# A delta-rule attention, a gated mixer and a channel mixer in one kernel: u blocks of w_in rounded in the second period, w_out and w_k later, mixing with delayed low parts

## Chip, cores, metric

The kernel runs on one core of one Trainium2 chip. The metric is the device time of one execution in microseconds (us). TensorE is called PE, VectorE DVE, ScalarE ACT, GpSimd POOL; SP only issues transfers here.

## What is computed

Three layers follow one another, for 4 sequences of 768 tokens and 384 channels (8 heads of 48). Cut to what matters:

```python
# 1: delta rule, token by token, per sequence and head
k_n = k / (np.linalg.norm(k, axis=-1, keepdims=True) + 1e-06)
for t in range(S):
    y[:, :, t] = einsum('bhd,bhde->bhe', q[:, :, t], state)
    v_old = einsum('bhde,bhd->bhe', state, k_n[:, :, t])
    state += beta[:, :, t] * einsum('bhd,bhe->bhde', k_n[:, :, t], v[:, :, t] - v_old)
# 2: x is y as (4, 768, 384); u, v halves of 512
u, v = split(gelu(x @ w_in))
v_s = einsum('ts,bsd->btd', w_sg, layernorm(v) * g_ln) + b_sg[None, :, None]
x = x + (u * v_s) @ w_out
# 3: x_prev is x one token earlier
k = relu((mu_k * x + (1 - mu_k) * x_prev) @ w_k)
r = sigmoid((mu_r * x + (1 - mu_r) * x_prev) @ w_r)
out = r * ((k * k) @ w_v)
```

## The kernel before, in words

**Products in two parts.** From the second layer on, each matrix is split into a high part (rounded to the type that PE multiplies) and a low part (the remainder), and a product is three matmuls: high by high, high by low, low by high (`mm3`, line 151). The weights arrive as pairs of 32-bit words. `narrow` (from line 154) makes a block of them into numbers: a load into one of three `raw` buffers (SP, line 160), a conversion on ACT (line 164), four bit operations on DVE into one of two `na` buffers (lines 169, 171, 173, 175, here called the rounding), an addition on POOL (177); `split` then copies the high part on ACT (120) and subtracts on POOL (123). The two `na` buffers come free when the subtraction is done. Six blocks of 128x256 belong to the v half of w_in and six to the u half; they stay on the chip. The blocks of w_out (eight, 192 wide) and w_k (twelve, 256 wide), later of w_r and w_v, are put back to memory in rounded form and read again in the third layer or the mixing.

**First layer.** Twelve steps `s` of 64 tokens are done in six groups, the periods; two steps each, and each step in two halves `o` of the channels. A period needs a triangular solve, `solver(g)` (lines 358 to 440), nearly all on DVE; it ends with a transpose into `DT` (line 440) and runs one period ahead of its use. `couple` (line 456) is PE's first product with `DT`; behind it come `st_d` (line 521, which also needs DVE's `residual`, line 475), ACT's copy `u` (526), `st_n` (534), and `st_rq`, `st_s`, `st_y` (498, 549, 563). ACT copies between them (540, 555), and 513 with a selection on POOL (514); `st_y` ends in ACT's copy `yst` (568) and six stores into `xT` (583, 588). The second layer's x @ w_in runs between the steps as `fill` (635 for v, 687 for u); where there is none, `keep_warm` issues matmuls without use (726).

**Who orders the work.** PE, ACT, DVE and POOL run in the order in which the program is written out until the third layer begins; SP's order is set by a scheduler up to the mixing. In the first layer a planner writes the order: a period has 24 ticks (`point[0]` counts them, from 0 after the first solve). `tick` starts jobs (a job is the rounding of one block): a `while` as long as more than `n_rest` jobs, that is blocks of w_in, remain and fewer than RUN[0] run, and an `if` for one job every EVERY ticks with at most RUN[1] running. `background` deals out the DVE time of a tick (BUDGET) among layer norm, solver and jobs in the ratio SHARE[point[1]]; each stream pays its time divided by its share.

**Mixing.** For four sequences and two halves `t` of the tokens, a slice `d` (of four) is 18 matmuls (line 960) into one PSUM bank, two operations on DVE (1056, 1058) and a split into `gh`, `gl`; `project` (1064) multiplies with w_out. `side(n)` works off up to n steps of the remaining rounding jobs; up to three run, a new one from the turns in `starts` on (a turn is a slice). Between the slices `load_v` splits the next sequence's v into the ring that PE reads.

Of the kernel before, what the change touches and what calls it, by code (L numbers as in the profile page):

```python
# [7 lines left out]
F32 = mybir.dt.float32  # L8
# [3 lines left out]
AF = mybir.ActivationFunctionType  # L12
ALU = mybir.AluOpType
# [23 lines left out]
PRE = 0.8  # L37
GRAM0 = 7
SOLVE0 = 1
RUN = (3, 2, 3)  # L40
SUMS = (0,)
EVERY = 6
LATE = 100
PUT = 2
JLAG = 2
# [9 lines left out]
LASTP = 134  # L55
# [2 lines left out]
COST = dict(rq=1.05, d=0.8, n=0.8, s=0.85, y=1.1)  # L58
INST = dict(rq=128, d=128, n=64, s=64, y=64)
PACE = 0.0157  # L60
SHARE = ((1, 12, 1), (1, 4, 1), (2, 8, 2))
NRAW = 3
NNA = 2
PD = 2
SD = 1
CS = (5, 4)
VF = (0, 3)
VD = 1
# [18 lines left out]
def fused_kernel(  # L87
# [18 lines left out]
    V, A, G, T = nc.vector, nc.scalar, nc.gpsimd, nc.tensor  # L106
# [10 lines left out]
    def split(eng_hi, eng_lo, src, hi, lo):  # L117

        if eng_hi is A:
            A.activation(hi, src, AF.Copy)  # L120
        else:
            eng_hi.tensor_scalar(hi, src, 1.0, None, op0=ALU.mult)
        eng_lo.tensor_tensor(lo, src, hi.bitcast(F32), op=ALU.subtract)  # L123
# [69 lines left out]
    def scratch(dram, name, nblk, n, cw=CW, pool=stg):  # L193

        d = dp.tile([nblk, P, 2, n], F32, name=name + "_d")

        def job(i, j):
            parts = []
            yield from narrow(dram, i, j, None, None, cw, pool, parts=parts)

            def put():
                nc.sync.dma_start(out=d[i, :, :, j:j + cw], in_=parts[0])

            yield PUT, put

        return d[:, :, 0], d[:, :, 1], [lambda i=i, j=j: job(i, j) for i in range(nblk) for j in range(0, n, cw)]
# [12 lines left out]
    wo_dh, wo_dl, jobs = scratch(w_out, "wo", 4, DM, DM // 2)  # L219
    wk_dh, wk_dl, j1 = scratch(w_k, "wk", 3, FF)  # L220
    jobs += j1
    n_rest = len(jobs)
# [26 lines left out]
    with ExitStack() as at:  # L249
# [70 lines left out]
        def gram(g, parts=((0, 64),)):  # L320

            GL = GLs[g] = GLb[g % 3]

            def half(i, c0, c1, j):
                t = kT[2 * g + i // 2]
                if j == 0:
                    GDs["ps"] = bank()
                gps = GDs["ps"]
                for p in range(4 * j, 4 * j + 4):
                    u = (i % 2) * 8 + p  # L330
                    for h in range(2):
                        r = 64 * (1 - h)
                        T.matmul(gps[r:r + 32, p, c0:c1], lhsT=t[r:r + 64, u, 0:32],  # L333
                                 rhs=t[r:r + 64, u, c0:c1], start=True, stop=True)
                        T.matmul(gps[r + 32:r + 64, p, c0:c1], lhsT=t[r:r + 64, u, 32:64],  # L335
                                 rhs=vw2(t, r, 64, u * C + 32 - c0, [(-32, (c1 - c0) // 32), (1, 32)]),
                                 start=True, stop=True)
                if j:
                    for x, c in ((GD[:, :, 8 * i:8 * i + 8].rearrange("p j u -> p u j"), 0),
                                 (GL[:, 8 * i:8 * i + 8, :], 32)):  # L340
                        if c0 <= c < c1:
                            A.activation(x, gps[:, :, c:c + 32], AF.Copy, scale=-1.0)

            GDs[g] = GD
            return [[(0, lambda i=i, j=j, c=c: half(i, *c, j)) for j in range(2)]
                    for c in parts for i in range(4)]
# [248 lines left out]
        later, vstat, streams, point = [], {}, [], [0, 0]  # L595
# [132 lines left out]
        def background(t):  # L728

            for e in [e for e in later if e[0] <= point[0]]:  # L730
                later.remove(e)
                e[1]()
            while splits and x_split(*splits[0]):
                splits.pop(0)
            t += debt[0]
            debt[0] = 0
            while t > 0:
                ready = [e for e in streams if e[0] <= point[0]]
                if not ready:
                    return  # L740
                kinds = [[e for e in ready if e[2] == k] for k in ("ln", "solve")]
                kinds.append([e for e in ready if any(e[1] is j for _, j in running[:2])])
                if not any(kinds):
                    return
                k = min((k for k in range(3) if kinds[k]), key=lambda k: spent[k])
                for j in range(3):
                    if not kinds[j]:
                        spent[j] = max(spent[j], spent[k])
                e = kinds[k][0]
                try:  # L750
                    c = next(e[1])
                    if isinstance(c, tuple):
                        e[0] = point[0] + c[0]
                        if c[0] == 0:
                            c[1]()
                        elif c[1] is not None:
                            after(c[0], c[1])
                    else:
                        t -= c
                        spent[k] += c / SHARE[point[1]][k]  # L760
                    streams.remove(e)
                    streams.append(e)
                except StopIteration:
                    streams.remove(e)
                    running[:] = [r for r in running if r[1] is not e[1]]
            debt[0] = min(t, 0) * (point[1] > 0)

        running, debt = [], [0]
        jobs = in_jobs + jobs
        n_jobs = len(jobs)  # L770

        def start_job(lead=LJ):
            j = jobs.pop(0)()
            running.append((n_jobs - len(jobs) - 1, j))
            next(j)
            streams.append([point[0] + lead, j, "job"])
# [58 lines left out]
        def tick():  # L835
            g, n = divmod(point[0], 24)
            point[1] = min(g, 1) + 1
            gg, nn = divmod(point[0] - GRAM0, 24)
            if nn == 0 and 0 <= gg and gg + 2 < NG:
                grams.extend(gram(gg + 2))  # L840
            if n == 0 and g + 1 < NG:
                streams.append([point[0] + SOLVE0, solver(g + 1), "solve"])
            late = point[0] >= LATE
            if point[0] < LASTP and jobs and len(running) < RUN[1 + late] and n % (2 if late else EVERY) == 0:
                start_job(LJ5 if late else LJ)
            background(BUDGET * (B0 if g == 0 else 1))
            while len(jobs) > n_rest and len(running) < RUN[0]:
                start_job()
            if grams and (point[0] - GRAM0) % GSTEP == 0:
                for _, f in grams.pop(0):  # L850
                    f()
                used[0] += 1.1
                dense[0] += 1
            point[0] += 1
# [152 lines left out]
    wr_dh, wr_dl, j2 = scratch(w_r, "wr", 3, DM, DM, st)  # L1007
    wv_dh, wv_dl, j3 = scratch(w_v, "wv", 8, DM, DM, st)
    jobs += j2 + j3
    live, turns, starts = [], [0], [1 + 2 * i for i in range(NRAW)]  # L1010

    def side(n):

        while n > 0:
            while jobs and any(x <= turns[0] for x in starts):
                starts.remove(next(x for x in starts if x <= turns[0]))
                j = jobs.pop(0)()
                next(j)
                live.append([turns[0] + 2, j, None])
            e = next((e for e in live if e[0] <= turns[0]), None)  # L1020
            if e is None:
                return
            if e[2]:
                e[2]()
            e[2] = None
            c = next(e[1], None)
            if c is None:
                live.remove(e)
                starts.append(turns[0] + 1)
            elif isinstance(c, tuple) and c[0]:  # L1030
                e[0], e[2] = turns[0] + 1, c[1]
            elif isinstance(c, tuple):
                c[1]()
            else:
                n -= 1

    halves = [(b, t) for b in range(B) for t in range(2)]
    us, gs = {}, {}
# [7 lines left out]
    def mix(b, t, d):  # L1046
        sl = slice(t * DM, t * DM + DM)
        pt, c0 = begun.pop(d, (None, 0))
        if pt is None:
            pt = ps.tile([P, HF], F32, name="ms")  # L1050
        for c in range(c0, 6):
            mix_mm(pt, b, t, d, c)
        if d == 0:
            gs[b, t] = [mp.tile([P, 4, DM], F32R, name=x) for x in ("gh", "gl")]
        w = vr.tile([P, DM], F32, name="w", bufs=2)
        V.scalar_tensor_tensor(w, pt[:, :DM], g_sb[:, d:d + 1], b_sb[:, sl],
                               op0=ALU.mult, op1=ALU.add)
        V.tensor_tensor(w, w, us[b, t][:, d], op=ALU.mult)  # L1058
        side(1)
        split(A, V, w, gs[b, t][0][:, d], gs[b, t][1][:, d])  # L1060
        side(SD)
        turns[0] += 1

# [173 lines left out]
```

## Time and profile before

| | us |
|---|---|
| median of 3 runs | 755.34 |
| lowest and highest run | 751.11, 757.25 |
| the profiled execution | 752.32 |
| its span in the profile | 750.3 |
| PE busy in the span | 690.7 (92%) |
| DVE, ACT, POOL busy | 510.8, 368.8, 202.4 |

All rows are from one profiled execution; their times count from the span's start. The execution's own time is 2 us above the span and 3.0 below the median. PE stood for 750.3 - 690.7 = 60 us of the span.

### The profile page before, as it was taken

The numbers are of one execution on the slowest core, as the hardware profiler recorded it, in microseconds if no ns is written. First come the engines' busy times: TensorE is split into PE (matmuls) and PEld (weight loads), VectorE is DVE, ScalarE is ACT, GpSimd is POOL, SyncE is SP. The second block draws the span as 40 slices with busy tenths as digits, with TensorE's granted clock in tenths as the row PEclk, the third lists the DMA queues.
The fourth block names the chain that finished last, engine by engine and source line by source line (L and its number), as shares of the span: only waits on it lengthen the run. The fifth ranks groups of instructions, "written<-read, shape, count | busy, mean of one in ns | idle before, by whom it ended". The sixth has DMA issues, their size and how long they took to land.

```text
span 750.3 us, 24940 instructions
## 1 busy us (share of the span) xinstructions
PE 690.7 (92%) x10832; PEld 640.4 (85%) x10832; DVE 510.8 (68%) x1070; ACT 368.8 (49%) x752; POOL 202.4 (27%) x253
## 2 busy tenths in 40 slices
PE   2568789999898999899989999999999999999998
PEld 2536568878776887779989999999999999999997
DVE  6989999878988795632494949489556564563341
ACT  2226656777666666874232313148445454452240
POOL 3033534454445355453133414420000000000000
PEclk9988989999999999999999999999999999999999
DMA  8503542674555565758755454195000000000000
GB/s 249 118 30 84 140 112 81 178 207 139 147 179 152 162 179 169 223 148 240 240 175 190 127 168 148 66 278 141 33 11 21 32 12 22 22 11 31 12 22 32
DMA packets 81549, 88.75 MB, mean 118 GB/s; under 512 B 24704, under 2 KB 64320, under 8 KB 81440
## 3 DMA queue, kind: packets, MB, share of 16 engines
q1 hardware_dynamic: 76384, 77.72, 35.1%
q0 software_dynamic: 5056, 9.44, 4.6%
q8 instruction: 85, 1.39, 0.8%
q14 instruction: 24, 0.20, 0.1%
HBM read 56.60 MB, written 25.82 MB: 110 GB/s over the span
## 4 chain that ended last, share of the span: by engine, by line
PE 73%; DVE 16%; DMA 4%; issue 3%; POOL 1%; SPq 1%; ACT 1%; POOLq 0%; DVEq 0%; ACTq 0%
PE ms L151 38%; PE ms L960 11%; PE ms L687 6%; PE ms L635 5%; DVE sg L355 4%; DVE sg L393 2%; PE ms L563 2%; PE rk L521 2%; PE sps L549 2%; PE ms L456 2%; PE rk L534 1%; PE rk L498 1%; PE ms L333 1%; PE ms L726 1%; DVE Yt L393 1%
## 5 line engine op out<-in xcount | busy, mean ns | idle before, releaser
L177 POOL TENSOR_TENSOR na<-na,raw 128x256 int32<-128x256 int32 (+2 forms) x43 | 36.4, 846 | 121.6 <-DVE na L175 53.5
L151 PE MATMUL ms<-wvh,sl 128*128 128x384 f32 x192 | 64.6, 336 | 0.0
L151 PE MATMUL ms<-wvl,sh 128*128 128x384 f32 x192 | 64.5, 336 | 0.0
L151 PE MATMUL ms<-wvh,sh 128*128 128x384 f32 x192 | 64.5, 336 | 0.0
L151 PE MATMUL ms<-xm_hi,sw0h 128*128 128x384 f32 x192 | 64.2, 335 | 0.0
L151 PE MATMUL ms<-xm_hi,sw0l 128*128 128x384 f32 x192 | 64.2, 334 | 0.0
L151 PE MATMUL ms<-xm_lo,sw0h 128*128 128x384 f32 x192 | 64.2, 334 | 0.0
L120 ACT ACTIVATE gh<-w 128x384 fp32r<-128x384 f32 x32 | 16.8, 525 | 94.9 <-DVE w L1058 94.9
L123 DVE TENSOR_TENSOR sl<-sg,sh 128x384 fp32r<-128x384 f32 x64 | 35.7, 558 | 30.2 <-ACT sh L120 30.2
L960 PE MATMUL ms<-sw0h,g 128*128 128x384 f32 x192 | 50.6, 336 | 3.0 <-ACT g L120 2.1
L120 ACT ACTIVATE sh<-sg 128x384 fp32r<-128x384 f32 x64 | 33.5, 524 | 35.9 <-DVE sg L1157 35.9
L960 PE MATMUL ms<-ws1h,g 128*128 128x384 f32 x192 | 49.9, 334 | 0.0
L355 DVE TENSOR_TENSOR sg<-sg,Yt 128x512 f32<-128x512 f32 (+10 forms) x78 | 46.7, 599 | 1.8
L1173 DVE TENSOR_TENSOR sg<-sg,ms 128x384 f32<-128x384 f32 x24 | 13.3, 554 | 45.3 <-PE ms L151 45.3
L1157 DVE TENSOR_TENSOR sg<-sg 128x384 f32<-128x384 f32 x64 | 35.5, 554 | 10.9 <-ACT sg L1156 10.9
L1156 ACT ACTIVATE sg<-ms 128x384 f32<-128x384 f32 x64 | 30.8, 481 | 23.7 <-PE ms L151 22.9
L514 POOL TENSOR_SCALAR_AFFINE_SELECT SQ<-SQ 64x512 f32<-64x512 f32 x36 | 27.5, 763 | 52.9 <-ACT SQ L513 51.7
L335 PE MATMUL ms<-kT 64*32 64x64 f32 (+1 forms) x640 | 23.3, 235 | 17.9 <-issue 17.9
L687 PE MATMUL ms<-xl,wiu_hi 128*128 128x256 f32 x144 | 39.7, 297 | 0.0
L687 PE MATMUL ms<-xh,wiu_lo 128*128 128x256 f32 x144 | 38.6, 291 | 0.9 <-issue 0.9
L333 PEld LDWEIGHTS ms<-kT 64*32 64x32 f32 x640 | 20.0, 131 | 22.2 <-issue 14.5
L120 ACT ACTIVATE xm_hi<-sg 128x384 fp32r<-128x384 f32 x48 | 23.3, 516 | 31.4 <-PE ms L151 30.5
(246 smaller groups left out, 2237.8 us busy)
## 6 DMA issues: line engine op xcount, KB each, us to landing
u_d<-ug SPq DMA_DIRECT2D x24, 256.0 KB, 3.8
u<-u_d SPq DMA_DIRECT2D x16, 384.0 KB, 4.6
vn_d<-v SPq DMA_DIRECT2D x22, 256.0 KB, 2.8
vk<-in_vk_dram SPq DMA_DIRECT2D x24, 192.0 KB, 4.0
vk<-in_vk_dram SPq DMA_DIRECT2D x12, 384.0 KB, 4.8
out_dram<-sg SPq DMA_DIRECT2D x24, 192.0 KB, 1.9
kT<-in_kt_d_dram SPq DMA_DIRECT2D x8, 512.0 KB, 5.8
SQ<-in_q_d_dram SPq DMA_DIRECT2D x36, 96.0 KB, 4.1
```

The costliest lines, as they stand in the source:

```text
L120: A.activation(hi, src, AF.Copy)
L123: eng_lo.tensor_tensor(lo, src, hi.bitcast(F32), op=ALU.subtract)
L151: T.matmul(pt, lhsT=a, rhs=b, start=(i == 0), stop=(i == n - 1))
L177: G.tensor_tensor(a.bitcast(I32), a.bitcast(I32), w_lo.bitcast(I32), op=ALU.add)
L333: T.matmul(gps[r:r + 32, p, c0:c1], lhsT=t[r:r + 64, u, 0:32], rhs=t[r:r + 64, u, c0:c1], start=True, stop=True)
L355: V.tensor_tensor(tv, vw(a_t, a_off, a_dims), vw(b_t, b_off, b_dims), op=ALU.mult)
L514: G.affine_select(out=pt, in_=pt, pattern=[[0, 8], [1, C]], compare_op=ALU.is_gt, fill=0.0, base=0, channel_multiplier=-1)
L635: T.matmul(vstat[g, b], lhsT=a[:, c], rhs=w[:, c], start=first, stop=last)
L687: T.matmul(vstat["u"][:, 2 * P * d:2 * P * d + 2 * P], lhsT=w[:, c, ds_], rhs=a[:, c].rearrange("p b t -> p (b t)"), start=first, stop=last)
L960: T.matmul(pt[:, :DM], lhsT=v[:, ds_], rhs=w, start=(c == 0 and i == 0), stop=(c == 5 and i == 2))
L1156: A.activation(r, pt[:, :DM], AF.Relu)
L1157: V.tensor_tensor(r, r, r, op=ALU.mult)
```

## The change

The u blocks of w_in are held back until tick 16 (the `while` keeps six jobs more until then); blocks of w_out and w_k start in the third period at the earliest, one every five ticks, with up to three jobs running. In the first period the solver's share rises from 4 to 8. In the mixing the high part is copied by ACT at once, the low part of a slice is subtracted one slice later (at once at the last slice of a sequence's second half), no rounding stands inside a slice any more, two steps of it stand behind each, and its first jobs start at turns 3, 4 and 6.

```diff
--- before.py
+++ after.py
@@ -37,9 +37,9 @@
 PRE = 0.8
 GRAM0 = 7
 SOLVE0 = 1
-RUN = (3, 2, 3)
+RUN = (3, 3, 3)
 SUMS = (0,)
-EVERY = 6
+EVERY = 5
 LATE = 100
 PUT = 2
 JLAG = 2
@@ -58,11 +58,11 @@
 COST = dict(rq=1.05, d=0.8, n=0.8, s=0.85, y=1.1)
 INST = dict(rq=128, d=128, n=64, s=64, y=64)
 PACE = 0.0157
-SHARE = ((1, 12, 1), (1, 4, 1), (2, 8, 2))
+SHARE = ((1, 12, 1), (1, 8, 1), (2, 8, 2))
 NRAW = 3
 NNA = 2
 PD = 2
-SD = 1
+SD = 2
 CS = (5, 4)
 VF = (0, 3)
 VD = 1
@@ -841,10 +841,10 @@
             if n == 0 and g + 1 < NG:
                 streams.append([point[0] + SOLVE0, solver(g + 1), "solve"])
             late = point[0] >= LATE
-            if point[0] < LASTP and jobs and len(running) < RUN[1 + late] and n % (2 if late else EVERY) == 0:
+            if g > 1 and point[0] < LASTP and jobs and len(running) < RUN[1 + late] and n % (2 if late else EVERY) == 0:
                 start_job(LJ5 if late else LJ)
             background(BUDGET * (B0 if g == 0 else 1))
-            while len(jobs) > n_rest and len(running) < RUN[0]:
+            while len(jobs) > n_rest + (0 if point[0] > 15 else 6) and len(running) < RUN[0]:
                 start_job()
             if grams and (point[0] - GRAM0) % GSTEP == 0:
                 for _, f in grams.pop(0):
@@ -1007,7 +1007,7 @@
     wr_dh, wr_dl, j2 = scratch(w_r, "wr", 3, DM, DM, st)
     wv_dh, wv_dl, j3 = scratch(w_v, "wv", 8, DM, DM, st)
     jobs += j2 + j3
-    live, turns, starts = [], [0], [1 + 2 * i for i in range(NRAW)]
+    live, turns, starts, owing = [], [0], [3, 4, 6], []
 
     def side(n):
 
@@ -1026,7 +1026,7 @@
             c = next(e[1], None)
             if c is None:
                 live.remove(e)
-                starts.append(turns[0] + 1)
+                starts.append(turns[0])
             elif isinstance(c, tuple) and c[0]:
                 e[0], e[2] = turns[0] + 1, c[1]
             elif isinstance(c, tuple):
@@ -1056,8 +1056,14 @@
         V.scalar_tensor_tensor(w, pt[:, :DM], g_sb[:, d:d + 1], b_sb[:, sl],
                                op0=ALU.mult, op1=ALU.add)
         V.tensor_tensor(w, w, us[b, t][:, d], op=ALU.mult)
-        side(1)
-        split(A, V, w, gs[b, t][0][:, d], gs[b, t][1][:, d])
+        A.activation(gs[b, t][0][:, d], w, AF.Copy)
+        if owing:
+            owing.pop()()
+        owing.append(lambda h=gs[b, t][0][:, d], l=gs[b, t][1][:, d]: V.tensor_tensor(
+            l, w, h.bitcast(F32), op=ALU.subtract))
+        if t == 1 and d == 3:
+            side(1)
+            owing.pop()()
         side(SD)
         turns[0] += 1
 
```

DVE, the end of solver 1: line 440 gives `couple` its operand, line 475 is the residual for `st_d` of step 2, line 360 begins solver 2; 169 to 175 on `na` are rounding. Before:

```order
L393 TENSOR_REDUCE sg_110<-sg_111 128x4x16
L173 TENSOR_SCALAR na<-na 128x256
L440 STREAM_TRANSPOSE DT<-sg_110 128x32x32
L169 TENSOR_SCALAR na<-raw 128x256
L175 SCALAR_TENSOR_TENSOR na<-raw,na 128x256
L475 TENSOR_TENSOR r_1642<-vk,rk 128x384
L171 TENSOR_SCALAR na<-na 128x256
L173 TENSOR_SCALAR na<-na 128x256
L175 SCALAR_TENSOR_TENSOR na<-raw,na 128x256
L360 STREAM_TRANSPOSE sg_108<-sg_109 128x1024
L364 TENSOR_SCALAR ss<-sg_108 128x32
```

Now, from line 440 to the same residual:

```order
L440 STREAM_TRANSPOSE DT<-sg_110 128x32x32
L171 TENSOR_SCALAR na<-na 128x256 x2
L173 TENSOR_SCALAR na<-na 128x256 x2
L175 SCALAR_TENSOR_TENSOR na<-raw,na 128x256 x2
L169 TENSOR_SCALAR na<-raw 128x256
L171 TENSOR_SCALAR na<-na 128x256
L173 TENSOR_SCALAR na<-na 128x256
L175 SCALAR_TENSOR_TENSOR na<-raw,na 128x256
L169 TENSOR_SCALAR na<-raw 128x256 x2
L171 TENSOR_SCALAR na<-na 128x256 x2
L173 TENSOR_SCALAR na<-na 128x256 x2
L475 TENSOR_TENSOR r_1634<-vk,rk 128x384
```

Two rounding instructions stood between lines 440 and 475; now there are 16. In the whole of solver 1 ahead of line 440 there were 21, and 4 are left. Behind the residual follow two 175, then 169, 171 and 173 of the last u block, and line 360.

SP, the same place: loads `raw` are weight blocks, the four kinds of `xT<-yst` are stores of `st_y` of step 1. Before, and then now:

```order
L160 DMA raw<-in_w_in_dram 128x512
L160 DMA raw<-in_w_out_dram 128x384
L279 DMA SQ_123<-in_q_d_dram 48x8x64
L279 DMA SQ_124<-in_q_d_dram 48x8x64
L583 DMA xT<-yst 48x6x128 x2
L588 DMA xT<-yst 32x2x128
L588 DMA xT<-yst 16x2x128 x2
L588 DMA xT<-yst 32x2x128
L160 DMA raw<-in_w_out_dram 128x384 x2
```

```order
L267 DMA kT_96<-in_kt_d_dram 128x1024
L279 DMA SQ_123<-in_q_d_dram 48x8x64
L279 DMA SQ_124<-in_q_d_dram 48x8x64
L583 DMA xT<-yst 48x6x128 x2
L588 DMA xT<-yst 32x2x128
L588 DMA xT<-yst 16x2x128 x2
L588 DMA xT<-yst 32x2x128
L160 DMA raw<-in_w_in_dram 128x512 x3
L160 DMA raw<-in_w_out_dram 128x384 x2
```

The loads of the last three u blocks have moved behind the stores.

DVE in the mixing of the first sequence, second half, from its second slice's 1056 to the first addition of `project`; `gl` is the low part, `g<-stw` a ring piece. Before, and then now:

```order
L1056 SCALAR_TENSOR_TENSOR w<-ms,g_sb,b_sb 128x384
L1058 TENSOR_TENSOR w<-w,u 128x384
L169 TENSOR_SCALAR na<-raw 128x384
L123 TENSOR_TENSOR gl<-w,gh 128x384
L171 TENSOR_SCALAR na<-na 128x384
L123 TENSOR_TENSOR g_7054<-stw,g_7054 128x512
L1056 SCALAR_TENSOR_TENSOR w<-ms,g_sb,b_sb 128x384
L1058 TENSOR_TENSOR w<-w,u 128x384
L173 TENSOR_SCALAR na<-na 128x384
L123 TENSOR_TENSOR gl<-w,gh 128x384
L175 SCALAR_TENSOR_TENSOR na<-raw,na 128x384
L1072 TENSOR_TENSOR xT<-xT,ms 128x384
```

```order
L1056 SCALAR_TENSOR_TENSOR w<-ms,g_sb,b_sb 128x384
L1058 TENSOR_TENSOR w<-w,u 128x384
L1062 TENSOR_TENSOR gl<-w,gh 128x384
L169 TENSOR_SCALAR na<-raw 128x256
L171 TENSOR_SCALAR na<-na 128x256
L123 TENSOR_TENSOR g_7032<-stw,g_7032 128x512
L1056 SCALAR_TENSOR_TENSOR w<-ms,g_sb,b_sb 128x384
L1058 TENSOR_TENSOR w<-w,u 128x384
L1062 TENSOR_TENSOR gl<-w,gh 128x384
L173 TENSOR_SCALAR na<-na 128x256
L175 SCALAR_TENSOR_TENSOR na<-raw,na 128x256
L1078 TENSOR_TENSOR xT<-xT,ms 128x384
```

Subtractions of `gl` are those of the slice before, and no rounding stands between a slice's product and its subtraction.

## Rows read from the trace of the kernel before

**Rows 1.** Timeline of PE: start, duration, line, operation, [stand before it, released by]

```profile
95.19 1.03 PE L456 MATMUL ms<-DT,sw0h 32*32 32x32 f32 x31 [4.71 <-DVE na L169]
...
193.27 0.92 PE L456 MATMUL ms<-DT,sg 32*32 32x32 f32 x47 [2.02 <-DVE DT L440]
...
242.06 1.20 PE L456 MATMUL ms<-sw0l,sw0h 32*32 32x32 f32 x64 [2.92 <-DVE sw0l L440]
...
394.12 0.45 PE L960 MATMUL ms<-sw0h,g 128*128 128x384 f32 x1 [2.08 <-ACT g L120]
...
395.62 0.62 PE L960 MATMUL ms<-sw0h,g 128*128 128x384 f32 x2 [0.88 <-DVE g L123]
```

**Rows 2.** Chain of waits, in order of time: start, duration, what

```profile
95.19 1.92 PE ms L456 x64
...
98.93 1.34 PE rk L521 x64
...
103.18 0.80 PE rk L534 x32
...
106.04 1.13 PE ms L456 x64
...
111.85 0.81 PE rk L521 x64
...
496.14 250.66 PE ms L151 x1440
```

**Rows 3.** Windows: PE, PEld, DVE, ACT, POOL busy, granted clock, DMA share

```profile
80.00:100.00 20.00, 14.94 (x446) 10.38 (x444) 19.69 (x31) 10.49 (x23) 11.57 (x14) 0.83 0.48 129
```

**Rows 4.** Timeline of DVE around the end of solver 1

```profile
88.06 1.27 DVE L169 TENSOR_SCALAR na<-raw 128x256 uint32<-128x256 uint32 x1
...
93.14 1.91 DVE L440 STREAM_TRANSPOSE DT<-sg 128x1024 f32<-128x1024 f32 x1
...
94.89 0.27 DVE L169 TENSOR_SCALAR na<-raw 128x256 uint32<-128x256 uint32 x1
...
95.41 0.54 DVE L475 TENSOR_TENSOR r<-vk,rk 128x384 f32<-128x384 f32 x1
...
96.88 0.42 DVE L175 SCALAR_TENSOR_TENSOR na<-raw,na 128x256 uint32<-128x256 uint32 x1
...
97.22 1.24 DVE L360 STREAM_TRANSPOSE sg<-sg 128x1024 f32<-128x1024 f32 x1
...
108.70 0.54 DVE L475 TENSOR_TENSOR r<-vk,rk 128x384 f32<-128x384 f32 x1
```

**Rows 5.** Timeline of ACT (two rows) and POOL (three rows), same place

```profile
88.22 0.58 ACT L568 ACTIVATE yst<-ms 128x512 f32<-128x512 f32 x1
...
100.40 0.49 ACT L526 ACTIVATE u<-rk 128x384 f32<-128x384 f32 x1 [0.16 <-ACT sw0h L459]
...
87.70 1.47 POOL L465 TENSOR_TENSOR vk<-vk,neT 128x768 f32<-128x768 f32 x1
...
95.63 0.73 POOL L177 TENSOR_TENSOR na<-na,raw 128x256 int32<-128x256 int32 x1 [1.84 <-issue]
...
96.88 1.01 POOL L123 TENSOR_TENSOR wiu_lo<-na,wiu_hi 128x256 fp32r<-128x256 f32 x1 [0.53 <-ACT wiu_hi L120]
```

**Rows 6.** Timeline of SP; issues of weight loads: count, size, us to landing

```profile
93.06 2.58 SPq L588 DMA_DIRECT2D xT<-yst  x4
...
raw<-in_w_in_dram SPq DMA_DIRECT2D x12, 256.0 KB, 4.0
```

**Rows 7.** Timeline of DVE, solver 3

```profile
178.12 0.43 DVE L355 TENSOR_TENSOR sg<-sg,Yt 128x256 f32<-128x256 f32 x1
...
189.36 0.24 DVE L173 TENSOR_SCALAR na<-na 128x192 uint32<-128x192 uint32 x1
```

**Rows 8.** Timeline of DVE, end of the first sequence's mixing

```profile
385.86 1.45 DVE L173 TENSOR_SCALAR na<-na 128x384 uint32<-128x384 uint32 x1
...
391.79 0.61 DVE L1056 SCALAR_TENSOR_TENSOR w<-ms,g_sb,b_sb 128x384 f32<-128x384 f32 x1
```

## The prediction

> **What bounds the kernel now.** I read the stretches in which PE (TensorE) stood still first, then the chain of waits, the granted clock, and last the engine that released each stand. [rows 1] are the five stands that matter: before the first `couple` of the second period (95.19, stand of 4.71 us, released by DVE), before that of the fourth (2.02) and of the fifth (2.92), and twice at the end of the first sequence's mixing (2.08 and 0.88). Behind the last of them PE hardly waits: the chain's longest piece runs from 496.14 for 250.66 us on PE [rows 2]. So PE sets the end, and a change of the order on DVE, ACT, POOL and SP is worth only what it does to PE's stands and to PE's clock. The sum is therefore over stands: those removed, and those that come in their place.
>
> The stand at 95.19 costs more than its 4.71 us. The stretch 80 to 100 has a granted clock of 0.83 [rows 3], and what follows the stand is slow: `couple` takes 1.92 us there against 1.13 at 106.04, the product `st_d` 1.34 against 0.81 at 111.85, and the four warming matmuls between (97.11 to 98.93) 1.82, which at the ratio of `couple` would be 1.07 [rows 2]. 0.79 + 0.53 + 0.75 = 2.1 us.
>
> **The change part by part.**
>
> *Rounding leaves solver 1.* The order shows 21 rounding instructions (four for a 128x256 block) between the triangular solver's instructions before, 4 after: 17 fewer ahead of the transpose at line 440 that gives `couple` its operand. One of them takes 0.27 to 0.42 us when it has DVE to itself, and 1.27 in the row at 88.06 [rows 4], which lies in POOL's 1.47 us at 87.70 [rows 5]. At the quiet mean of a block, (3 x 0.27 + 0.42) / 4 = 0.31, 17 x 0.31 = 5.3 us, or 17 x 1.27 = 21.6 at the most. I take 7, near the quiet rows. DVE ended line 440 at 93.14 + 1.91 = 95.05 [rows 4]; it now ends near 88, at the latest at 95.05 - 5.3 = 89.8. PE was free at 95.19 - 4.71 = 90.48. So all 4.71 us of this stand go, for any value in that range.
>
> *The six u blocks come in a burst behind line 440.* Before, two rounding instructions stood between line 440 and the first residual (line 475) that PE's next `st_d` needs; now 16 stand there, the last three steps of blocks A and B, C whole, and the first three of D and E. Worked through from 88: A and B six instructions, 2 x (0.27 + 0.27 + 0.42) = 1.9, to 89.9. C needs a buffer `na` that A gives back only when POOL has added (0.73), ACT copied (about 0.5, the stand before POOL's row at 96.88) and POOL subtracted (1.01) [rows 5]: 92.1, and C ends at 93.3. D and E need raw loads. Those stood on SP ahead of the six stores of the transposed output; now they stand behind them. The stores need ACT's copy `yst`, which ended at 88.80 [rows 5] and comes about 0.8 us earlier without two rounding instructions ahead of it. Four of the six stores took SP 2.58 us, so six some 3.9 [rows 6]: 88.0 + 3.9 = 91.9, and a raw load lands 4.0 us after its issue [rows 6]: D 95.9, E 96.2. E's first step and two pairs more, 5 x 0.27 = 1.4, bring line 475 to about 97.6 and, 0.54 later, `st_d` to 98.1. It began at 98.93 [rows 2]. PE then is 0.8 us early instead of 6.8, having stood still for over 5 us at this place (from 92.7, when `couple` at 90.5 and the warming matmuls are done, 1.1 + 1.1), one product later; I count its clock afterwards as low as before.
>
> *What is queued behind D and E.* On ACT, their conversions (line 164) wait for the loads and stand ahead of the copies of line 540, 513 and of `u` (line 526). On POOL the addition for D stands behind the causal selections that need line 513. ACT: conversions to 96.8, line 540 and two of 513 to 99.0, POOL selection to 99.7, D added 100.4, copied 100.9, subtracted 101.7. ACT's `u` comes near 103.4, against 100.40 [rows 5], which is ahead of PE's `st_n` at 103.18 [rows 2] no longer: +0.4. DVE can round F only with D's buffer, so solver 2's first transpose (line 360) goes from 97.22 [rows 4] to about 102.0, and everything behind it by 4.8: the residual at 108.70 to 113.5. PE's `st_d` that needs it began at 111.85 [rows 2]; it starts at 113.6. So at this point the net of the first two parts is **+1.8 us**: the stand of 4.71 has moved behind the burst, and the burst lasts longer than the room before it. From both sides: if nothing of the burst reached PE, -4.7 - 2.1 = -6.8; if each of the eight POOL instructions of the burst held up a DVE instruction as at 88.06 (1.27 instead of 0.27, +1.0 [rows 4]), +1.8 + 8 = +9.8. I keep both for the range.
>
> *Period 1.* The w_out blocks (16 rounding instructions) leave solver 2. PE had no stand there worth counting, so this gives nothing but lets DVE make up its 4.8 us. If it doesn't, the third `couple` is late; 16 x 0.31 = 5.0 says that it does.
>
> *Solvers 3 and 4.* Behind the last residual before line 440 there now stand, in solver 3, one rounding step (0.24) and one 128x256 step (0.43) more [rows 7], and in solver 4 one rounding step. PE waits for line 440 there already (2.02, 2.92), so these lengthen the stands: +0.7 + 0.2 = **+0.9**.
>
> *Mixing.* Before, DVE ran each slice as two products, wait for ACT's rounded copy, subtraction, with rounding in between. It fell behind: the first product of the last slice began at 391.79, and the rounding row at 385.86 took 1.45 beside POOL [rows 8]; ACT and DVE then were late with the fourth ring piece and PE stood 2.08 + 0.88 [rows 1]. Now the subtraction is done one slice later, so it finds ACT's copy ready, and 7 rounding instructions instead of 11 stand ahead of the last slice. A slice is then three instructions of about 0.6 us, less than PE's 18 matmuls, and DVE waits for PE. Both stands go: **-2.96**. Bounds: -2.96 and, if the ring piece stays as late, 0. The same work follows in the second sequence with a slice's delay; PE had no stand there, and I count 0.
>
> *The rest.* From the sixth solver to the mixing, and in the last stage, the order is the same: 0.
>
> Sum: +1.8 + 0.9 - 2.96 = **-0.3 us** on the profiled execution's 752.32, so 752.0. The median of the runs shown is 3.0 above that execution; the forecast in their measure is 755.0.
>
> The Trainium skill, page "SBUF — State Buffer", section "Who interferes with whom", says that DVE and GpSimd share one pair of ports under an exclusive lock, so that a DVE instruction in a two-port mode waits for the whole of a GpSimd instruction. The 1.27 against 0.27 in [rows 4] agrees. By it the burst, which sets POOL's twelve instructions for the u blocks right beside DVE's rounding, is the worst place for them; it would make of the sum what the third case below says.
>
> **The rivals.**
> *Burst hidden (faster).* The raw loads land early enough, or ACT and POOL are quicker than worked out, so that line 475 comes before PE has done `couple` and its warming matmuls, and solver 2 has slack. For it: DVE is free from 88 on, and PE needs its residual only at about 92.7. Against it: a load issued behind the stores can't land before 95. Price -6.8 + 0.9 - 2.96 = -8.9: 746.
> *Burst blocked (slower).* POOL's additions and subtractions hold up DVE's steps one for one, +8 on top of the sum: 763. It makes the kernel slower from the first of these eight on. For it: DVE is busy 19.69 of the 20 us of [rows 3], with POOL at 11.57. Against it: most of DVE's time at this place is waiting for loads, and there POOL costs nothing.
> *The mixing's stands stay.* The change doesn't do what it should there, since the ring piece hangs on the loads or on POOL: +1.8 + 0.9 = +2.7: 758.
>
> **How the numbers follow.** Forecast 0.60, burst hidden 0.17, mixing unchanged 0.15, burst blocked 0.08. One per cent, 7.5 us, is about what a measurement of this kernel can tell from no change: below 747.8 and above 762.9. Of the burst-hidden case most, 0.14, lies below; of the blocked case 0.06 lies above; the rest, 0.80, between. The range goes to the first case's 746 and stops at 761, short of the blocked case.
>
> **What would show it.** Right: no stand before the first `couple` of period 2, a stand of about 5.5 us before the `st_d` behind it, released by DVE's line 475, raw loads landing after 95, solver 2's line 360 near 102; no stand at the end of the first sequence's mixing; 0.7 and 0.2 more before `couple` 4 and 5. Wrong: `st_d` at 93 to 94 with a clock near 1 (burst hidden), or several DVE steps of over 1 us behind line 440 (blocked), or PE standing for the fourth ring piece (mixing).

## The result, and the profile after

The changed kernel takes 763.25 us (median of 4 runs, 761.37 to 765.76) against 753.43 for the kernel before (4 runs; the fourth, 751.53, has lowered the 755.34 that the forecast was counted in): ratio 1.0119, with a 95% interval of 1.008 to 1.0158. It is some 1% slower, clear of the noise, and outside the forecast range of 746 to 761. Its profiled execution took 761.78 us with a span of 760.1, 9.8 above the span of before.

How PE stands, by the timeline of PE in the changed kernel (start, duration, operation, in brackets the stand before it and what released it):

```profile
99.95 1.50 PE L521 MATMUL rk<-r,DT 32*32 32x48 f32 x64 [5.33 <-DVE r L475]
...
106.14 0.87 PE L534 MATMUL rk<-u,sw0h 32*32 32x48 f32 x32 [0.88 <-ACT u L526]
...
118.99 1.26 PE L521 MATMUL rk<-r,DT 32*32 32x48 f32 x52 [4.79 <-DVE r L475]
...
200.88 1.20 PE L456 MATMUL ms<-DT,sg 32*32 32x32 f32 x64 [0.85 <-DVE DT L440]
...
220.65 0.37 PE L563 MATMUL ms<-sw0h 128*64 128x64 f32 x1 [3.56 <-ACT GL L342]
...
254.30 1.92 PE L456 MATMUL ms<-sw0l,sw0h 32*32 32x32 f32 x64 [2.71 <-DVE sw0l L440]
```

The stand of 4.71 us of [rows 1] before the first `couple` of the second period is gone, but two stands, of 5.33 and 4.79 us, have come before the two `st_d` products behind it, both released by DVE's residual (line 475), and one of 0.88 before `st_n`. At 220.65 there is a stand of 3.56, released by ACT, which has no counterpart before. The stands of 2.02 and 2.92 of [rows 1] are 0.85 and 2.71. In the mixing PE has none left.

The windows, with the columns of [rows 3] (PE, PEld, DVE, ACT, POOL busy, granted clock as a share of full speed, DMA share, GB/s):

```profile
80.00:100.00 20.00, 13.26 (x412) 8.99 (x410) 13.21 (x26) 9.66 (x22) 7.32 (x9) 0.92 0.52 138
100.00:120.00 20.00, 14.13 (x421) 11.28 (x425) 15.15 (x46) 12.02 (x23) 10.57 (x13) 0.84 0.47 128
120.00:140.00 20.00, 20.00 (x556) 17.48 (x545) 19.38 (x31) 10.86 (x22) 5.00 (x7) 0.90 0.19 48
119.00:123.00 4.00, 4.00 (x118) 3.79 (x119) 3.76 (x10) 1.46 (x3) 0.00 (x0) 0.50 0.02 4
125.00:140.00 15.00, 15.00 (x462) 12.98 (x460) 14.59 (x23) 8.31 (x18) 5.00 (x7) 1.00 0.25 63
```

PE is busy for 13.26 us where [rows 3] had 14.94, and the granted clock is below 1 in the three stretches of 20 us: 0.92 in the first ([rows 3]: 0.83), 0.84 in the second, 0.90 in the third. The last two lines show where: behind the second stand it is 0.50 (1.2 GHz, the lower of its two levels) from 119 to 123, and 1.00 from 125 on.

Setting PE's products of both traces beside one another gives where the 9.8 us came (start after minus start before): first `st_d` of the second period +1.1, its `st_n` +3.0, second `st_d` +7.2, second `st_n` +8.8, third `couple` +8.0, fourth +7.6, the `st_n` behind the stand at 220 +12.5, fifth `couple` +12.2, last `st_n` of the first layer +13.4. Then the mixing takes back 4.1: from PE's first product of the mixing (336.75 before, 350.14 now) to the start of the chain's last long piece (496.14, 505.43), it lasts 155.3 instead of 159.4 us. So there are two losses, some 8.8 and 4.8 us, and one gain.

**The first loss.** SP, at the place where the loads of the last three u blocks had been moved behind the stores:

```profile
88.26 1.31 SPq L583 DMA_DIRECT2D xT<-yst  x2
...
89.62 3.77 SPq L588 DMA_DIRECT2D xT<-yst  x4
...
93.48 2.57 SPq L160 DMA_DIRECT2D raw<-in_w_in_dram  x3
```

The six stores take SP from 88.26 to 93.39, and the three loads are issued from 93.48 on. DVE:

```profile
85.76 2.00 DVE L440 STREAM_TRANSPOSE DT<-sg 128x1024 f32<-128x1024 f32 x1
...
97.48 0.29 DVE L169 TENSOR_SCALAR na<-raw 128x256 uint32<-128x256 uint32 x1 [4.12 <-DMA raw<-in_w_in_dram]
...
99.35 0.55 DVE L475 TENSOR_TENSOR r<-vk,rk 128x384 f32<-128x384 f32 x1
...
104.29 0.81 DVE L169 TENSOR_SCALAR na<-raw 128x256 uint32<-128x256 uint32 x1 [3.72 <-POOL wiu_lo L123]
...
105.67 1.24 DVE L360 STREAM_TRANSPOSE sg<-sg 128x1024 f32<-128x1024 f32 x1
...
108.49 1.65 DVE L138 TENSOR_TENSOR rn_t<-rn_y 128x32 f32<-128x32 f32 x1
...
118.39 0.54 DVE L475 TENSOR_TENSOR r<-vk,rk 128x384 f32<-128x384 f32 x1
```

Line 440 ends at 87.76: the solver is ready early enough. Then DVE waits 4.12 us for the load of the fourth block, and again 3.72 us for an `na` buffer before it can take the sixth; only then does solver 2 begin (105.67). POOL, behind that wait:

```profile
100.49 0.65 POOL L514 TENSOR_SCALAR_AFFINE_SELECT sw0h<-sw0h 64x512 f32<-64x512 f32 x1 [5.02 <-ACT sw0h L513]
...
102.27 0.73 POOL L177 TENSOR_TENSOR na<-na,raw 128x256 int32<-128x256 int32 x1
...
103.53 0.73 POOL L123 TENSOR_TENSOR wiu_lo<-na,wiu_hi 128x256 fp32r<-128x256 f32 x1 [0.53 <-ACT wiu_hi L120]
...
108.41 1.68 POOL L123 TENSOR_TENSOR xl<-xT,xh 128x768 fp32r<-128x768 f32 x1 [1.82 <-ACT xh L120]
```

Its selection for `st_rq` (line 514) comes when ACT, which had stood for the same loads, is through; the fourth block's addition and subtraction stand behind it, and DVE's row at 104.29 behind those. The last row of POOL, 1.68 us, has DVE's row of 1.65 us beside it, an instruction that takes 0.19 elsewhere in the same solver. But this is no part of the loss: in the kernel before, the same instruction of POOL (the low part of x, not of a weight block) had a slow row of solver 2 beside it, too (0.17 in the changed kernel):

```profile
103.69 1.75 POOL L123 TENSOR_TENSOR xl<-xT,xh 128x768 fp32r<-128x768 f32 x1 [3.61 <-ACT xh L120]
...
103.92 1.53 DVE L355 TENSOR_TENSOR sg<-sg,Yt 128x4 f32<-128x4 f32 x1
```

**The second loss.** ACT ahead of the stand at 220.65, and then SP with, as its last line, the same load in the chain of waits:

```profile
219.51 0.38 ACT L164 ACTIVATE raw<-raw 128x192 int32<-128x192 uint32 x1 [6.45 <-DMA raw<-in_w_out_dram]
...
220.18 0.42 ACT L342 ACTIVATE GL<-ms 128x256 f32<-128x256 f32 x1
```

```profile
207.51 1.99 SPq L583 DMA_DIRECT2D xT<-yst  x2
...
209.56 2.57 SPq L588 DMA_DIRECT2D xT<-yst  x4
...
214.86 0.57 SPq L160 DMA_DIRECT2D raw<-in_w_out_dram  x1
...
214.86 4.63 DMA raw<-in_w_out_dram
```

The conversion of a w_out block waits 6.45 us for its load. The copy into `GL` that PE's product needs stands behind it. The load was issued at 214.86 and landed 4.63 us later; ahead of it on SP stood, from 207.51 on and without a gap of note, the six stores of a `st_y`, two loads of `vk` and a store of `u_d`. So here, too, a weight load stands behind six stores.

### The profile page after: what moved, and what is told of

Its sections match the earlier page's. It is cut to its first block, busy times and chain, and to the rows that moved or that the text cites. A ratio compares the mean times of both kernels' runs of the same rounds, so it can differ in the third digit from the quotient of the medians.

```text
span 760.1 us, 24951 instructions
## 1 busy us (share of the span) xinstructions
PE 694.8 (91%) x10832; PEld 644.7 (85%) x10832; DVE 511.8 (67%) x1070; ACT 368.5 (48%) x752; POOL 203.0 (27%) x253
## 4 chain that ended last, share of the span: by engine, by line
PE 77%; DVE 10%; DMA 3%; issue 3%; ACT 3%; POOL 2%; SPq 2%; POOLq 0%; ACTq 0%; DVEq 0%
PE ms L151 38%; PE ms L960 13%; PE ms L687 5%; PE ms L635 5%; DVE sg L355 3%; PE ms L563 3%; DVE sg L393 2%; PE rk L521 2%; PE rk L534 2%; PE ms L333 2%; PE sps L549 2%; PE rk L498 2%; PE ms L456 1%; DMA raw<-in_w_in_dram 1%; PE ms L726 1%
## 5 line engine op out<-in xcount | busy, mean ns | idle before, releaser
L177 POOL TENSOR_TENSOR na<-na,raw 128x256 int32<-128x256 int32 (+2 forms) x43 | 38.5, 896 | 96.7 <-DVE na L175 38.5
L355 DVE TENSOR_TENSOR sg<-sg,Yt 128x512 f32<-128x512 f32 (+10 forms) x78 | 43.7, 561 | 2.0
L687 PE MATMUL ms<-xh,wiu_hi 128*128 128x256 f32 x144 | 38.6, 290 | 0.0
```

What stands on the lines that cost most here:

```text
L177: G.tensor_tensor(a.bitcast(I32), a.bitcast(I32), w_lo.bitcast(I32), op=ALU.add)
L355: V.tensor_tensor(tv, vw(a_t, a_off, a_dims), vw(b_t, b_off, b_dims), op=ALU.mult)
L687: T.matmul(vstat["u"][:, 2 * P * d:2 * P * d + 2 * P], lhsT=w[:, c, ds_], rhs=a[:, c].rearrange("p b t -> p (b t)"), start=first, stop=last)
```

## The experiments

Medians are given with those of the kernel before on the same chips, and the ratio with its interval.

**1. The mixing's part alone**, on the kernel before (all of the diff from `live, turns, starts` on, with SD = 2).

> The kernel before with the mixing's part of the change alone (low parts one slice later, no rounding inside a slice, jobs from turns 3, 4, 6). If the mixing's gain is its own: 3 to 4 us below before (about 750), no stand of PE at the end of the first sequence's mixing. If the gain came only because fewer blocks were left or the first layer ended later: no change against before (753).

748.77 against 753.2; ratio 0.9964 (0.993 to 0.9998), only just clear of 1. PE has no stand left in the mixing, which lasts 155.3 us as in the changed kernel (337.32 to 492.64). The mixing's gain is its own.

**2. The first layer's part alone** (SD = 1 and the mixing of before).

> The changed kernel with the mixing as before. If the two parts add up: 3 to 4 us above the changed kernel (about 767), with +13 us at the end of the first layer against before. If they don't: as the changed kernel (763).

768.04 against 753.2; ratio 1.0185 (1.0122 to 1.0247). By the medians the first layer loses 15 us (9 to 19 by the interval) and the mixing gives 4, so that the parts add within the noise. In this trace PE's first product of the mixing comes 16.4 us later than before, where 13 was expected; in the changed kernel, with the same first layer, it was 13.4.

**3. Two running jobs.**

```diff
-RUN = (3, 3, 3)
+RUN = (3, 2, 3)
```

> The changed kernel with at most two jobs running in the middle periods instead of three (RUN 3, 2, 3). If three running jobs on three raw buffers make a conversion on ACT wait for its load ahead of the copies that PE needs: the stand of 3.6 us before the product at 220 goes, and 4 to 5 us with it (about 758.5). If it is the later start or the denser rhythm of the w_out blocks: as the changed kernel (763).

775.6 against 753.2; ratio 1.0279 (1.0213 to 1.0345), so a miss. The stand at 220 did go: the distance to the kernel before is +8.3 us at the fourth `couple` and at the `st_y` in question. But 15 blocks were left for the mixing instead of 12, and PE stands elsewhere:

```profile
328.85 1.42 PE L521 MATMUL rk<-r,DT 32*32 32x48 f32 x59 [6.04 <-DVE r L475]
...
529.74 0.69 PE L151 MATMUL ms<-xm_hi,sw0h 128*128 128x384 f32 x1 [9.38 <-ACT xm_hi L120]
```

The first of these is a residual late at the end of the first layer; the second the start of the third layer, where the chain runs over the last loads and stores of w_v (3.67 us for the store `wv_d`) back to jobs that were done too late. In the changed kernel, with three blocks fewer left, PE has no such stand; that the blocks alone make the difference was not tested.

**4. Without the hold.**

```diff
-            while len(jobs) > n_rest + (0 if point[0] > 15 else 6) and len(running) < RUN[0]:
+            while len(jobs) > n_rest and len(running) < RUN[0]:
```

> The changed kernel with the u blocks started as before (no six kept back). 10 rounding instructions stand ahead of line 440 and 10 between it and the residual, and the loads of the fourth and fifth block stand ahead of the stores. If the loads behind the stores and the burst make the loss: the 8.8 us of the second period's start go, perhaps 2 to 3 more (752 to 755). If the loss is the solver's new share or the later w_out blocks: 760 to 763.

758.45 against 753.2; ratio 1.0079 (1.0043 to 1.0115), between the two expectations. PE, and the row of DVE ahead of solver 2:

```profile
97.08 1.18 PE L521 MATMUL rk<-r,DT 32*32 32x48 f32 x48 [2.87 <-DVE r L475]
...
115.66 0.61 PE L521 MATMUL rk<-r,DT 32*32 32x48 f32 x20 [3.67 <-DVE r L475]
...
217.67 0.27 PE L563 MATMUL ms<-sw0h 128*64 128x64 f32 x1 [3.47 <-ACT GL L342]
...
100.87 0.29 DVE L169 TENSOR_SCALAR na<-raw 128x256 uint32<-128x256 uint32 x1 [3.84 <-DMA raw<-in_w_in_dram]
```

The two stands are 2.87 and 3.67 instead of 5.33 and 4.79, so the hold made 3.6 of their 10.1 us, about a third. The rest stays with 12 rounding instructions between line 440 and the residual (not the 10 expected), and not by their number alone: the fourth and fifth block's loads are ahead of the stores, but the sixth block's was issued at 97.33, behind them, and DVE waits 3.84 us for it before solver 2 begins, at 102.20. With no wait for a load inside it, this burst also shows what POOL costs: its 12 rows add up to 6.5 us, where 12 at the quiet mean of 0.31 would be 3.7. The stand at 217 stays too.

**5. Loads ahead of the stores.** The order of PE, ACT, DVE and POOL is that of the changed kernel.

```diff
-                store_x(g, o, ysts[o])
+                if g:
+                    store_x(g, o, ysts[o])
+                else:
+                    after(2, lambda y=ysts[o]: store_x(g, o, y))
```

> The changed kernel with the first period's output stores written two ticks later: the order of PE, ACT, DVE and POOL is the same, only on SP the loads of the last three u blocks stand ahead of six stores instead of behind them. If those loads are what the residual waits for: the fourth and fifth block land near 93.8 and 95.7 instead of 97.5 and 98.3, the residual comes near 97.1 instead of 99.35, and 2 to 2.5 us go at once and again nothing later (about 761). If the loads were all of the loss: 755. If the burst on DVE and POOL alone holds the residual: 763.

760.39 against 752.74; ratio 1.008 (1.0052 to 1.0109), as the first case said. The profiled execution, 754.94, is the fastest of the ten, so the trace is read for places, not for its end. SP, DVE and PE (line 588 is 591 here):

```profile
89.07 4.81 SPq L160 DMA_DIRECT2D raw<-in_w_in_dram  x3
...
96.35 2.53 SPq L591 DMA_DIRECT2D xT<-yst  x4
...
95.83 0.55 DVE L475 TENSOR_TENSOR r<-vk,rk 128x384 f32<-128x384 f32 x1
...
101.63 1.24 DVE L360 STREAM_TRANSPOSE sg<-sg 128x1024 f32<-128x1024 f32 x1
...
114.70 0.55 DVE L475 TENSOR_TENSOR r<-vk,rk 128x384 f32<-128x384 f32 x1
...
96.43 1.39 PE L521 MATMUL rk<-r,DT 32*32 32x48 f32 x64 [1.47 <-DVE r L475]
...
115.31 0.94 PE L521 MATMUL rk<-r,DT 32*32 32x48 f32 x36 [4.31 <-DVE r L475]
```

The residual comes 3.5 us earlier, 2.6 if counted from line 440 (84.83 here, 85.76 in the changed kernel), and the first stand is 1.47 instead of 5.33. The second one stays at 4.31: line 360 begins at 101.63, still 4.4 behind [rows 4]; just ahead DVE waits 2.75 us for an `na` buffer.

**6. The conversion one tick later.**

```diff
-        yield 0, lambda: A.activation(w_lo.bitcast(I32), ...
+        yield 1 if dram is w_out else 0, lambda: A.activation(w_lo.bitcast(I32), ...
```

> The changed kernel with ACT's conversion of a w_out block one tick later, three jobs running as in the change and twelve left for the mixing. If the stand of 3.56 us at 220 is the conversion that waits for its load ahead of the copies PE needs: it goes, and 3.5 to 5 us with it (about 759). If the copies are late for another reason: 763.

759.89 against 752.74; ratio 1.0083 (1.0053 to 1.0113). ACT:

```profile
215.01 0.43 ACT L342 ACTIVATE GL<-ms 128x256 f32<-128x256 f32 x1
...
221.59 0.37 ACT L164 ACTIVATE raw<-raw 128x192 int32<-128x192 uint32 x1 [3.97 <-DMA raw<-in_w_out_dram]
```

The conversion still waits for its load, but the copy into `GL` is now ahead of it, and the stand at 220 is gone with three jobs running and twelve left for the mixing: it was the conversion's place on ACT, not the number of jobs in itself. That an earlier load would do the same was not tried.

**7 and 8. The two halves of the mixing's part**, each on the kernel before: the rounding moved and the low parts as before (7); the low parts a slice later and the rounding as before (8).

> The kernel before, in the mixing only the rounding moved (out of the slices, two steps behind each, later first jobs); low parts as before. If the rounding on DVE made the two stands: they go, -2.5 to -3 (about 750). If the wait for ACT's copy in each slice made them: 0 to -1.

> The kernel before, in the mixing only the low part subtracted one slice later; the rounding as before. If the wait for ACT's copy in each slice (0.3 to 0.8 us) made the two stands: they go, -2.5 to -3 (about 750). If the rounding made them: 0 to -1.

752.51 (0.999, 0.997 to 1.0009) and 751.43 (0.9979, 0.9952 to 1.0005), against 752.74: each half gives what was expected of it if the other made the stands, or little more, so neither made them alone. PE in 7, two of five stands that add up to 3.6 us (its profiled execution, 758.96, is the slowest of twelve):

```profile
396.40 0.44 PE L960 MATMUL ms<-sw0h,g 128*128 128x384 f32 x1 [0.56 <-ACT g L120]
...
475.40 0.44 PE L960 MATMUL ms<-sw0h,g 128*128 128x384 f32 x1 [1.42 <-ACT g L120]
```

and in 8, both of its stands:

```profile
380.61 0.45 PE L151 MATMUL ms<-gl,wo_hi 128*128 128x384 f32 x1 [0.95 <-DVE gl L1063]
...
396.99 0.62 PE L960 MATMUL ms<-sw0h,g 128*128 128x384 f32 x2 [1.82 <-DVE g L123]
```

2.96 us of stands before become 3.6 and 2.8 with one half, 0 with both, and the mixing lasts 162.3 and 158.6 us against 159.4 before and 155.3 with both. The times alone don't tell this, as the intervals of 1, 7 and 8 overlap. With the order alone DVE still waits for ACT in each slice (0.59 us in the slices ahead of 396.40), and with the low parts alone the rounding still stands ahead of the ring piece; that each is enough to make DVE late is read from these two traces.

**9. The solver's share 8 alone**, with the mixing's part, on the kernel before.

```diff
-SHARE = ((1, 12, 1), (1, 4, 1), (2, 8, 2))
+SHARE = ((1, 12, 1), (1, 8, 1), (2, 8, 2))
```

> The kernel before with the mixing's part and the solver's share 8 alone: no blocks kept back, w_out as before. 10 rounding instructions ahead of line 440, 10 between it and the residual, loads ahead of the stores. If any rounding moved from ahead of line 440 to behind it comes back as a stand at the two residuals: like the run without the hold, stands of about 3 and 3.5 us before the two products, 4 to 5 us at that place lost against before, and about 753 after the mixing's gain. If only the hold did harm: 744 to 746, since the stand of 4.7 us goes.

753.21 against 752.69; ratio 0.9991 (0.9965 to 1.0017): about the first case. PE waits in three places instead of one (the profiled execution, 755.97, is the slowest of the ten):

```profile
98.23 0.88 PE L521 MATMUL rk<-r,DT 32*32 32x48 f32 x64 [2.99 <-DVE r L475]
...
106.14 1.35 PE L534 MATMUL rk<-u,sw0h 32*32 32x48 f32 x32 [1.90 <-ACT u L526]
...
117.25 0.88 PE L521 MATMUL rk<-r,DT 32*32 32x48 f32 x64 [1.93 <-DVE r L475]
```

The sum of 2.99, 1.90 and 1.93 takes the place of 4.71, without any hold, and by the medians the mixing's gain is used up; the interval overlaps that of experiment 1. As in experiment 4, 12 rounding instructions stand behind line 440, not 10, and the sixth block's load (98.81) stands behind the stores: DVE waits 4.45 us for it ahead of solver 2, which begins at 103.95. So this run doesn't part the number of instructions from the order of the loads.

**10. A share of 5**, in the same way.

> The kernel before with the mixing's part and the solver's share 5: 18 rounding instructions stay ahead of line 440, 5 stand between it and the residual. PE's product behind it had some 3 us of slack in the trace of before. If that slack takes five instructions: the stand before the coupling product falls from 4.7 to about 3, none appears behind it, 1 to 2 us below the mixing's part alone (747 to 748). If the next solve is what is late: as the mixing's part alone (749) or above.

747.06 against 752.69; ratio 0.9924 (0.9895 to 0.9953): the fastest of all, though its interval overlaps that of experiment 1. PE:

```profile
93.25 0.92 PE L456 MATMUL ms<-DT,sw0h 32*32 32x32 f32 x47 [2.87 <-DVE DT L440]
...
102.50 0.87 PE L534 MATMUL rk<-u,sw0h 32*32 32x48 f32 x32 [1.62 <-ACT u L526]
```

The first stand is 2.87 instead of 4.71 (3.70 to 3.88 in experiments 1, 7 and 8, whose first layer has the order of before). None stands before the `st_d` behind it, and 1.62 before `st_n`, which was not expected: ACT's `u` there waits behind its work for a u block. At the first product of the mixing this trace is level with that of before (+0.06), so that the shorter stand reaches the end is not shown.

**11. Both repairs**, 5 and 6 together, on the changed kernel.

> The changed kernel with both repairs: loads ahead of the stores, and the w_out conversion one tick later. If the two causes are separate: both gains add, 6 us below the changed kernel (757), with stands of about 1.5 and 4.3 us left before the two products and none at 220. If not separate: 760.

756.56 against 752.69; ratio 1.0055 (1.0034 to 1.0075): the gains add, 6.7 us below 763.25, and the interval lies just below the changed kernel's, which those of 5 and 6 overlap. The stands before the two `st_d` are 3.11 (1.5 expected) and 4.58; at 220.30 one of 1.06 is left, released not by `GL` but by ACT's `v`.

**12. The sixth block behind the head of solver 2**, on experiment 5; PE's and SP's order stay.

```diff
-                start_job()
+                start_job(LJ if len(jobs) > n_rest + 1 or point[0] < 16 else 6)
```

> The kernel of the run with the loads ahead of the stores, and in it the last u block's conversion, rounding, addition and split moved behind the head of solver 2 (the order of PE and SP is the same). If the last block's wait for a buffer of na holds back solver 2 and so the second residual: line 360 comes near 98 instead of 102, the residual near 111 instead of 115, the stand of 4.3 us before the second product shrinks below 1, and 3 to 5 us go (about 757 against 760.4). If solver 2's own length sets the second residual: no change (760).

757.32 against 753.67; ratio 1.0049 (1.0017 to 1.008). DVE:

```profile
98.56 1.23 DVE L360 STREAM_TRANSPOSE sg<-sg 128x1024 f32<-128x1024 f32 x1
...
112.20 0.55 DVE L475 TENSOR_TENSOR r<-vk,rk 128x384 f32<-128x384 f32 x1
```

Solver 2 begins at 98.56 instead of 101.63 and its residual comes at 112.20 instead of 114.70. The stand of 4.31 us before the second product is gone; its `st_n` begins 3.4 us after that of the kernel before, in experiment 5 it was 5.2. A stand of 2.98 us that the profile puts down to issue (it shows nothing that PE waited for) lies just ahead of it in this execution, so the gain at this place can be read no finer. Solver 2 took 13.6 us to its residual, 13.1 in experiment 5 and 11.5 in [rows 4], so its own length has a part as well. The interval overlaps that of experiment 5.

## Why the prediction was wrong

- *Rounding leaves solver 1*: right. Line 440 ended at 87.76 (about 88 forecast) and the 4.71 us went. *One product later*: right in kind. The burst came, the loads stood behind the stores, PE stood 5.33 us (over 5 forecast), and the residual waited for them.
- *The step that failed first* is the size of +1.8 us for the burst; at the same product it measured +7.2, and +8.8 by the `st_n` behind it. Its terms were short one by one. The stores: "88.0 + 3.9 = 91.9" was 88.26 + 5.13 = 93.4 (four of the six took 3.77 instead of the 2.58 of [rows 6], a row near the low end: the first layer of before has such groups of four from 2.52 to 3.61); the loads landed 97.5 and 98.3 instead of 95.9 and 96.2. That alone moved `st_d` from 98.1 to 99.95. The wait on POOL: the fourth block's addition came at 102.27, where I had it done at 100.4, and `u` at 105.62 instead of 103.4. Solver 2 began at 105.67 (102.0 forecast), and then took 12.7 us to the residual instead of the 11.5 that I carried over from [rows 4]. The last step of the sum also left out the residual's own 0.54: 113.5 + 0.54 is 114.0, not 113.6, so by its own terms it came to +2.2. The clock: I put its price on the first stand only; behind the second one it is 0.50 from 119 to 123, `st_d` took 1.50 us against 0.81 [rows 2], and PE fell back by another 1.6 us (7.2 to 8.8).
- The rival *burst blocked* (the prediction's "third case", second in its list) named 763, and 763.25 was measured, but that is chance. In solver 2 DVE's row of 1.65 us beside POOL's 1.68 is 1.46 above its usual 0.19. The page "SBUF — State Buffer" of the Trainium skill, section "Who interferes with whom", has this for a DVE instruction with two inputs in SBUF beside a GpSimd instruction that reads SBUF, and the trace agrees. But POOL's instruction there is not of the burst, and before it held a row of 1.53. Of the burst's own, the sixth block's addition and subtraction have rows of 0.66 and 0.60 beside them (110.17, 111.54; 0.19 each otherwise), and before there was one of 0.73 (99.15): a net +0.3 us. Inside the burst three of DVE's rows, of 0.81 to 0.83 (91.04, 92.53, 104.29), are 0.4 to 0.5 above their quiet time, and DVE waits for loads and buffers there anyway. So it is a small part of the 8.8 us; where the loads come in time, as in experiment 4, it is more.
- *Period 1*: right in that no new stand came there and the third `couple` had none, so DVE did make up its delay. PE's distance fell from 8.8 to 6.6 in it, 1.0 of it at places where the trace of before has stands put down to issue and the other one shorter ones (0.91 against 0.18 us at the same u product, 1.22 against 0.94 at the same `st_y`); I take that for variation, not for a gain, and the rest has no cause shown.
- *The second step that failed* is one I left out: for the w_out blocks, moved to the third period and denser, I followed DVE's rounding alone ("Solvers 3 and 4") and not their conversions on ACT and loads on SP, which so stood at nothing in the sum. That cost 4.8 us at 220 (experiment 6). The +0.9 that I did count there came on DVE (from the last residual to the start of line 440 10.44 us against 9.48 in solver 3, 9.87 against 9.58 in solver 4), but not as a stand: the two were 0.85 and 2.71, together 1.4 shorter than before. That fits with PE itself coming later: it has a stand of 1.43 put down to issue at 192.36, which the trace of before has not, and one of 1.13 at 246.52, where before has 0.64.
- *Mixing*: right. -2.96 forecast; the stands went and the stage is 4.1 us shorter, of which 2.96 are stands; of the other 1.1, 1.0 is PE's own busy time, 156.28 us before and 155.29 now for the same 903 matmuls in windows over the mixing, whose cause is not shown. That both halves of the edit are needed (7, 8) I had not said.
- The sum, by what was measured: 8.8 - 2.2 (period 1) + 1.4 (a stand put down to issue at 192) + 4.8 + 0.6 (the rest to the end of the first layer) - 4.1 = +9.3 at the start of the third layer's long piece, 9.8 in the span.

What stays open: by the medians, the edits of 5, 6 and 12 give back 2.9, 3.4 and 3.1 us, 9.4 of the 15 that experiment 2 puts on the first layer (13.4 in the changed kernel's trace), each uncertain by some 3 us (my estimate from the intervals of the runs). By the medians experiment 9 puts some 4 on the share of 8, but its interval overlaps that of experiment 1, and a load behind the stores is in it. The three repairs together were not run, nor the share of 8 with all loads in time. The 1.4 us at 192 and the 2.98 in experiment 12 have no releaser in the profile.

## What to carry to other kernels

Work that is taken out of one engine's way ahead of a wait is still ahead of the next wait: count how much room the product behind has (some 3 us here, which held five rounding instructions; twelve and sixteen did not fit), and move no more than that. Count with them what they wait for: with its loads ahead of the stores (experiment 5) the burst of sixteen still took 9.0 us from the end of line 440 to the residual, where 16 at 0.31 would be 5.0, since DVE waits for `na` buffers that POOL gives back. When a block of work is moved, follow every queue that it passes, its load on the issuing queue and its small conversion on ACT above all: an instruction that waits for a transfer holds whatever is written behind it on its engine. The second loss was of this kind, and a part of the first (experiment 5). A stage's gain can need two edits at once, so test the halves before calling either of them the cause.

## What the runs showed of the hardware

The same order of the first layer on all engines brought the first product of the mixing at 336.75, 337.32, 338.90 and 340.84 us in four profiled executions (the kernel before and experiments 1, 8 and 7). From 60 us on, stands of 0.2 to 2.2 us that the profile puts down to issue differ among them: some are there in one or two only, some at the same product with another length (1.09, 0.49, 0.76 and 0.56 us before the product of line 335 that starts at 109.28 in the kernel before). A difference of 2 us between two traces' ends therefore says little here. A stand with a named releaser is there at the same product in each of the four, but its length moves, too: 4.71, 3.88, 3.70 and 3.75 us before the first `couple` of the second period, 2.02, 1.74, 0.79 and 1.56 before that of the fourth, 2.92, 3.09, 3.58 and 2.24 before that of the fifth. So a stand that comes or goes says much, and one that is a microsecond longer or shorter little.
